# Attention and two MLPs on one core: another order for the opening, and two joins of the first MLP rearranged

## The chip, the cores and the metric

The kernel runs on one core of a Trainium2 chip. The metric is the device time of one execution in microseconds (us), lower is better. It is one program: the time starts before the first load and ends with the last store.

## What is computed

Attention over 4 batches of 8 heads, 576 positions, head width 64, with a bias from a running sum; then a first MLP with a leaky activation (a slope alpha per hidden unit), then a second MLP with a squared relu. The result of each feeds the next.

```
scores = scale * q @ k.T
cum    = cumsum(maximum(s, 0))                       # over the sequence
scores = where(causal, -1e9, scores + minimum(-(cum_i - cum_j), 0))
attn   = exp(scores - max) / (sum + 1e-9)
x      = (attn @ v) as 2304 x 512
h = x @ w_in  (512 -> 2048);  g = maximum(h, 0) + alpha * minimum(h, 0);  y = g @ w_out  (2048 -> 512)
h = y @ w_in2 (512 -> 2048);  g = maximum(h, 0) ** 2;                     out = g @ w_out2
```

## The kernel before

**Number format.** Every fp32 operand of a matmul is split into a rounded part `hi` and a rest `lo` (`hi` L323, `lo` L335 for q and k; L985 and L986, L624, L610, L668, L1369 and L1370, L1417 and L1418 elsewhere). A product is the sum of three matmuls (hi*hi, hi*lo, lo*hi; the table `TERMS`). So each tile that TensorE reads has been made by one instruction for hi (mostly ScalarE or GpSimd) and one for lo (mostly VectorE or GpSimd).

**Attention.** The 16 pairs of heads run as a pipeline. For a pair: `load_qk`, split, transposes on TensorE into the bank `ps_tr` (`pp` L344 for a head of q or k, 4 transposes each; `pp_tail` L369 for the last 64 positions; in a later pair two `pp` stand together as 8), evacuation to QS, QM (q, scaled), KS, KH (k) by ScalarE or VectorE, scores by `qk` (L412; row tile i and head h, operations `qk_ih`; matmuls L419, L420, L425), `red` on VectorE (L446: mask and row maximum), `exp` on ScalarE (L459), transposes of the probabilities (`tr`, L527), and two products with v (L561, L577). The score matmul of 66 rows (L420) reads, beside k, two rows of KH that hold the running sum `cum`; they come by a DMA, for pair 0 straight from the split sum `cum_hl` (tile `pt`), for later pairs by way of the DRAM tensor `cumD`.

**Opening.** L691 to L772 write the order of pair 0's loads, splits, transposes and evacuations by hand, with the splits of pair 1 (raw_q_132, raw_k_133 in the order rows; pair 0 has raw_q_123, raw_k_124). `s` arrives in the tile `prl`; `cum` is a relu (L711) and a scan (L712) on VectorE. `init_persistent` (L269) zeroes the tail columns of QM, QS and other tiles: for pair 0 on VectorE (L271 to L273, and the memset of `cum` L710) and partly GpSimd, for pair 1 on GpSimd. `keep_warm` (L696) issues filler matmuls of zeros (tile `iv`) into the bank `ps_xa`; they compute nothing that is used. From pair 0's scores on, the table `PIPE` gives each operation a slot in a pair, `RAMP` shifts operations of the first (and last) pairs by fractions of a pair, `WARM` puts filler matmuls of 256 columns ahead of operations of pair 0. The sum of slot and shift sorts all operations, and `in_order` chains the instructions of each engine in that order.

**First MLP.** Three passes over thirds of the 2304 rows (768 each, in halves of 384). Passes 0 and 1 are steps 0 to 15 and 16 to 31: a step makes 128 hidden units (`mlp_mm` L637; activation and split `mlp_act` L658 to L668 in tiles gg and gs) and adds their share of the outputs (`mlp_parts` L922, matmuls L935, in four portions of six matmuls, one called a chunk here). The third pass, `pass_of_seven` (L1373), makes 2 x 2 blocks by seven products instead of eight (L1440, a product is six matmuls; z = 0 to 6 counts them, q = 0 to 7 the groups), and places one chunk behind each product:

```
                in_order(IN_ORDER[:1])
                if (q<7) or (z>1):
                    chunk()
                in_order(IN_ORDER[:1])
```

The chunks of group q = 0 are still the outputs of steps 30 and 31. The third pass needs sums of x (tile xc, split at L985 and L986, differences L1020, handed out as `handed` steps) and sums of weights. These weight sums (`prep_sums` L181 to L184, `prep_first` L196 to L199, and the conversions `prep_conv` L133 to L142) are a list of tasks `todo` that is dealt out over the steps by `spans`, triples of first step, last step and share of the tasks' cost (L964).

## Time and profile before

| | |
|---|---|
| runs, us | 950.13, 950.86 (median), 954.41 |
| profiled execution, us | 952.03 |
| its span, us | 950.2 |
| mean granted TensorE clock | 1.000 |
| TensorE busy | 936.9 us, 99% of the span |

The span counts from the first to the last instruction, the profiled execution 1.9 us more. Times in the views are counted from the start of the span. A row of a timeline gives start and busy time; consecutive equal instructions stand in one row with their count; in brackets the idle time ahead of it and what ended that.

### The profile page before, as it was taken

How to read it: one execution, taken by the hardware profiler on the slowest of the kernel's cores; microseconds unless marked ns; L12 is line 12 of the kernel's file. 1: busy time of each engine (PE TensorE's matmuls, PEld its weight loads, DVE VectorE, ACT ScalarE, POOL GpSimd, SP SyncE). 2: the span in 40 equal slices, each digit the busy share in tenths (PEclk: the TensorE clock that was granted, in tenths of full speed). 3: DMA queues.
4: the chain of work that ended last, by engine and by line, in shares of the span. 5: the costliest groups of instructions: out<-in, count | busy, mean ns of one | idle time of the engine just before them, and what ended most of it. 6: DMA issues, size and time to landing. Idle time of an engine off the chain costs nothing.

```text
span 950.2 us, 16991 instructions
## 1 busy us (share of the span) xinstructions
PE 936.9 (99%) x5909; PEld 882.6 (93%) x5909; DVE 770.4 (81%) x1446; ACT 607.1 (64%) x1272; POOL 280.3 (29%) x278
## 2 busy tenths in 40 slices
PE   7999999999999999999999999999999999999998
PEld 6888888899999899999999999999999999999998
DVE  7788878868778987789778878788988888888685
ACT  6999988856566565577666656566445664456432
POOL 7466555134233212322102100344003530045200
PEclk9999999999999999999999999999999999999999
DMA  5787765337666758989568562586755867448384
GB/s 148 197 210 205 198 156 139 87 103 252 208 198 228 275 192 301 341 276 311 168 214 261 184 200 82 163 314 217 244 182 164 273 222 261 146 118 287 118 259 134
DMA packets 141063, 195.69 MB, mean 206 GB/s; under 512 B 50962, under 2 KB 102674, under 8 KB 135602
## 3 DMA queue, kind: packets, MB, share of 16 engines
q1 hardware_dynamic: 140384, 194.11, 65.1%
q8 instruction: 47, 0.77, 0.3%
q10 hardware_dynamic: 594, 0.50, 0.2%
q14 instruction: 38, 0.31, 0.1%
HBM read 140.47 MB, written 45.83 MB: 196 GB/s over the span
## 4 chain that ended last, share of the span: by engine, by line
PE 91%; DVE 3%; DMA 2%; ACT 1%; SPq 1%; issue 1%; POOL 0%; ACTq 0%; DVEq 0%; POOLq 0%
PE acc L1253 18%; PE po L935 18%; PE ph L637 12%; PE ph L1440 6%; PE a L1094 5%; PE b L1094 5%; PE c L1094 5%; PE ps_tr L527 5%; PE ps_xb L577 3%; PE d L1094 3%; PE ps_xa L561 2%; PE ps_sc L419 2%; PE ps_sc L420 2%; PE ps_tr L348 2%; PE ps_sc L425 2%; DMA raw_w<-in_moe_w_in_dram 1%
## 5 line engine op out<-in xcount | busy, mean ns | idle before, releaser
L1253 PE MATMUL acc<-th,w2s 128*128 128x384 f32 x1008 | 177.6, 335 | 0.0
L1253 PEld LDWEIGHTS acc<-th,w2s 128*128 128x128 f32 x1008 | 175.2, 188 | 0.0
L935 PE MATMUL po<-gs,wo_hi 128*128 128x512 f32 (+1 forms) x768 | 166.3, 336 | 0.7 <-DVE gs L1418 0.5
L935 PEld LDWEIGHTS po<-gs,wo_hi 128*128 128x128 f32 x768 | 122.8, 188 | 14.3 <-DVE gs L1418 1.1
L637 PE MATMUL ph<-xs,wi_hi 128*128 128x384 f32 x512 | 130.6, 335 | 2.1 <-DVE gg L664 1.9
L985 ACT CAST th<-g 128x768 fp32r<-128x768 f32 x84 | 70.2, 836 | 78.5 <-PE acc L1253 57.0
L986 DVE TENSOR_TENSOR th<-g,th 128x768 fp32r<-128x768 f32 x84 | 80.2, 955 | 24.8 <-ACT th L985 24.6
L935 PE MATMUL po<-gs,wo_lo 128*128 128x256 f32 (+1 forms) x384 | 99.1, 337 | 0.0
L637 PEld LDWEIGHTS ph<-xs,wi_hi 128*128 128x128 f32 x512 | 90.6, 188 | 4.0 <-DVE gg L664 2.7
L986 DVE TENSOR_TENSOR w1h<-w1f,w1h 128x512 fp32r<-128x512 f32 x96 | 74.3, 777 | 22.2 <-ACT w1h L985 22.0
L142 POOL TENSOR_TENSOR wc<-cv_t,wc 128x512 uint32<-128x512 uint32 x24 | 37.0, 1549 | 165.3 <-DVE cv_t L138 121.1
L637 PE MATMUL ph<-xs,wi_lo 128*128 128x384 f32 x256 | 85.6, 334 | 0.0
L985 ACT CAST w1h<-w1f 128x512 fp32r<-128x512 f32 x96 | 53.8, 565 | 39.6 <-PE b L1094 25.4
L446 DVE CUSTOM_DVE_ANT_0 pr<-ps_sc,mask 128x128 f32<-128x128 f32 (+3 forms) x128 | 61.8, 486 | 14.3 <-PE ps_sc L420 11.3
L142 POOL TENSOR_TENSOR wf<-cv_t,wf 128x512 uint32<-128x512 uint32 x32 | 45.2, 1413 | 94.3 <-DVE cv_t L138 71.0
L1105 POOL TENSOR_TENSOR g<-g 128x384 f32<-128x384 f32 x24 | 23.8, 990 | 162.2 <-ACT g L1104 162.1
L459 ACT ACTIVATE pr<-pr,nmax 128x128 f32<-128x128 f32 (+3 forms) x128 | 71.2, 557 | 0.4
L935 PEld LDWEIGHTS po<-gs,wo_lo 128*128 128x128 f32 x384 | 59.2, 188 | 7.9
L1094 PE MATMUL a<-xc,w1h 128*128 128x384 f32 x288 | 58.5, 335 | 0.0
L1440 PE MATMUL ph<-xc,wi_hi 128*128 128x384 f32 x224 | 57.6, 337 | 0.6 <-DVE xc L986 0.6
L1094 PE MATMUL c<-xc,w1h 128*128 128x384 f32 x288 | 58.0, 334 | 0.0
L1094 PE MATMUL b<-xc,w1h 128*128 128x384 f32 x288 | 57.8, 335 | 0.0
(204 smaller groups left out, 2130.2 us busy)
## 6 DMA issues: line engine op xcount, KB each, us to landing
w2s<-w2D SPq DMA_DIRECT2D x42, 1024.0 KB
w1f<-w1D SPq DMA_DIRECT2D x72, 256.0 KB
raw_w<-in_moe_w_in_dram SPq DMA_DIRECT2D x32, 512.0 KB
w2D<-whl SPq DMA_DIRECT2D x16, 896.0 KB
raw_w<-in_moe_w_out_dram SPq DMA_DIRECT2D x24, 512.0 KB
...
```

The lines of the kernel that those rows point to most:

```text
L142: nc.gpsimd.tensor_tensor(d, tt, d, ALU.add)
L446: nc.vector.tensor_tensor_reduce(o, banks.pop(("s", i, h))[:, :w], m, -1.0, first, ALU.add, ALU.min, nmax[:, h : h + 1])
L459: nc.scalar.activation(o, o, AF.Exp, bias=m, scale=-1.0, accum_out=sums_of[n][:, i, h : h + 1])
L527: last = nc.tensor.transpose(ps[:, z * P : (z + 1) * P], pr[:, c0 : c0 + P], ident)
L577: last = nc.tensor.matmul(xb[64 * h : 64 * h + 64, c0 : P + TAIL], vv[:, j, h, :], pt[:, h, j, c0:], start=(j == 0), stop=(j == 4),)
L637: nc.tensor.matmul(ph[h][:, :HT], ws[a][:, kb * P : (kb + 1) * P], xs[kb][:, bb, h * HT : (h + 1) * HT], start=(cnt == 0), stop=(cnt == 3 ...
L935: nc.tensor.matmul(acc, ws[a][:, m * P : (m + 1) * P], gs[:, bb, c_], start=first_ and z == 0, stop=lst and z == 2, skip_group_check=True,)
L985: a = nc.scalar.copy(dst[:, 0], src)
L986: v = nc.vector.tensor_sub(dst[:, 1], src, dst[:, 0].bitcast(F32))
L1094: nc.tensor.matmul(pt[:, :HT], hl[:, a, c0 + kb * P : c0 + (kb + 1) * P], xc[i][:, b, kb, :], start=(first and cnt == 0), stop=(cnt == 5), ...
L1253: nc.tensor.matmul(acc[m][:, :HT], ws[:, y, (2 * q + qq) % 4, m * P : (m + 1) * P], th[:, x, qq, :], start=(fresh and q == 0 and qq == 0 a ...
L1440: nc.tensor.matmul(acc[:, :HT], hl[a][:, c0 + kb * P : c0 + (kb + 1) * P], xp[i][:, b, kb, :], start=(fresh and cnt == 0), stop=(cnt == 5) ...
```

## The change

**1. The opening** is written in another order. The tails of q and k (64 positions) are loaded by DMAs of their own on ScalarE's queue, the main parts both on SyncE's queue (SP); k of pair 1 is loaded ahead of q; v of pair 0 ahead of the two rows of KH; the store to `cumD` goes to ScalarE's queue. The memsets of QM, QS and `cum` leave VectorE (three of them are GpSimd's; the scan starts from the zero tile). The splits of pair 0 are dealt out anew: hi of q, of k's second head and of k's tail on ScalarE, hi of k's first head on GpSimd; lo of k's first head, of k's tail and of q's heads on VectorE, lo of k's second head and of q's tail on GpSimd. The transposes of pair 0 run k, q, k, tails, q; three of the filler matmuls of 512 columns behind the first block go away, and one of the first block. GpSimd takes lo of pair 1's k before that of its q, with beta (L71, made from alpha) between them. In the diff, the long old sequence is left out; it is in the code above.

```diff
+    H0, H1, HT_ = slice(0, 4), slice(4, 8), slice(8, 9)
+    nc.vector.memset(zero, 0.0)
+    nc.gpsimd.memset(ptl[0][0:64, :, 4, :], 0.0)
+    load_main(0, 0, nc.sync)
+    nc.scalar.dma_start(s_sb, s.rearrange("b h c -> (b h) c"))
+    load_main(0, 1, nc.sync)
+    nc.vector.memset(warm, 0.0)
+    nc.gpsimd.memset(QM[0].bitcast(F32)[:, :, 0:TAIL], 0.0)
+    keep_warm(8)
+    nc.gpsimd.memset(raw_v[0][0:64, 4, :, :], 0.0)
+    nc.vector.tensor_scalar(s_sb, s_sb, 0.0, None, ALU.max)
+    load_tail(0, 0, nc.scalar)
+    nc.vector.tensor_tensor_scan(cum, s_sb, zeros, 0.0, ALU.add, ALU.add)
+    load_qk(1, 1, nc.sync)
+    load_tail(0, 1, nc.scalar)
+    nc.gpsimd.memset(QS[0].bitcast(F32)[:, :, 0:TAIL], 0.0)
+    hi(0, 1, 2, H0)
     hi(0, 0, 0, H0)
...
+    load_qk(1, 0, nc.sync)
+    hi(0, 1, 0, H1)
+    nc.scalar.copy(cum_hl[:, 0, :], cum)
+    hi(0, 1, 0, HT_)
+    keep_warm(1)
+    lo(0, 1, 1, H0)
+    nc.gpsimd.memset(QM[0].bitcast(F32)[64:66, :, TAIL:], 1.0)
+    load_v(0)
+    lo(0, 0, 1, H0)
+    pp(0, 1, 0)
+    nc.gpsimd.memset(rs_[0], 0.0)
+    hi(0, 0, 0, slice(4, 9))
     lo(0, 1, 2, H1)
+    lo(0, 0, 2, HT_)
+    nc.scalar.activation(warm, warm, AF.Exp)
+    pp(0, 0, 0)
+    pp(0, 1, 1)
+    nc.vector.tensor_sub(cum_hl[:, 1, :], cum, cum_hl[:, 0, :].bitcast(F32))
+    ks_out(0, 0)
+    nc.sync.dma_start(KH[0].bitcast(F32)[64:66, 0, :], cum_hl.bitcast(F32)[0 : 1])
+    hi(1, 1, 2)
+    hi(1, 0, 2)
+    keep_warm(2)
+    nc.scalar.dma_start(cumD, cum_hl.bitcast(F32))
...
+    lo(1, 1, 2)
+    load_alpha()
...
+    lo(1, 0, 2)
```

The engine operand of `hi` and `lo` is 0 for ScalarE, 1 for VectorE, 2 for GpSimd.

**2. RAMP and WARM** have new numbers: the shifts of most operations of pairs 0 to 2 and of some of pair 3 change by up to a pair and mostly by under a fifth of one. The fillers are now

```diff
-    WARM = {("qk_11", 0): 1, ("qk_20", 0): 2, ("qk_21", 0): 3, ("qk_30", 0): 3, ("qk_31", 0): 2, ("qk_40", 0): 2, ("tr_0", 0): 1, ("tr_1", 0): 1}
+    WARM = {('qk_20', 0): 4, ('qk_21', 0): 2, ('qk_30', 0): 2, ('tr_0', 0): 2, ('tr_1', 0): 4, ('qk_01', 0): 1, ('qk_00', 0): 1, ('pp_q0', 1): 1}
```

**3. The join of passes 0 and 1.** The spans of the weight tasks move a little, which takes one `prep_first` (four subtractions) from step 15 to step 17 and shifts single tasks in steps 18 to 22.

```diff
-    spans = ((13,14.3,.11),(16.6,29.2,.65),(33.5,43,.24))
+    spans = ((13, 13.9, 0.09), (16.3, 29.2, 0.67), (33.5, 43, 0.24))
```

**4. The join of pass 1 and the third pass.** In the last step (31) one more input step is issued ahead of the activation, and the chunks of group q = 0 stand otherwise: two behind product z = 0, one behind z = 1 and z = 3, the rest after the group.

```diff
+        if step == len(steps) - 1:
+            with tc.issue_after(anchor), tc.issue_after(anchor_v):
+                for _ in range(1):
+                    handed.pop(0)()
         gs, anchor, anchor_v = mlp_act(f, ph, step == 0)
...
-                if (q<7) or (z>1):
+                for _ in range(2*(z==0)+(z in(1,3)) if q==0 else int(q<7 or z>1)):
                     chunk()
```

**In the built order.** On TensorE at the very start, before the change (hl_q and hl_k are the split q and k, ps_xa the bank of the fillers, KS to QM the transposed operands of pair 0):

```order
L348 MATMUL ps_tr<-ident_r,hl_q 128x128 x4
L700 MATMUL ps_xa<-iv 128x512
L348 MATMUL ps_tr<-ident_r,hl_k 128x128 x4
L700 MATMUL ps_xa<-iv 128x512
L348 MATMUL ps_tr<-ident_r,hl_q 128x128 x4
L700 MATMUL ps_xa<-iv 128x512
L348 MATMUL ps_tr<-ident_r,hl_k 128x128 x4
L700 MATMUL ps_xa<-iv 128x512
L373 MATMUL ps_tr<-ident_r,hl_q 128x128
L373 MATMUL ps_tr<-ident_r,hl_k 128x128
L700 MATMUL ps_xa<-iv 128x512 x2
```

and after it:

```order
L348 MATMUL ps_tr<-ident_r,hl_k 128x128 x4
L348 MATMUL ps_tr<-ident_r,hl_q 128x128 x4
L348 MATMUL ps_tr<-ident_r,hl_k 128x128 x4
L700 MATMUL ps_xa<-iv 128x512 x2
L373 MATMUL ps_tr<-ident_r,hl_q 128x128
L373 MATMUL ps_tr<-ident_r,hl_k 128x128
L348 MATMUL ps_tr<-ident_r,hl_q 128x128 x4
L700 MATMUL ps_xa<-iv 128x512
L419 MATMUL ps_sc<-KS_121,QS_119 128x128
L420 MATMUL ps_sc<-KH_122,QM_120 128x128
L700 MATMUL ps_xa<-iv 128x256
```

The first head of k now stands ahead of q's, the first three blocks of transposes follow one another with no filler between, and the second head of q comes last.

On VectorE at the start, before (prl is s and then its running sum, pt the split sum, L726 and L318 evacuate):

```order
L692 MEMSET iv 128x576
L706 MEMSET warm 1x1
L271 MEMSET QM_120 2x2x576
L272 MEMSET QM_120 66x2x64
L273 MEMSET QS_119 128x2x64
L710 MEMSET prl 32x576
L711 TENSOR_SCALAR prl<-prl 32x576
L712 SCALAR_TENSOR_TENSOR prl<-prl 32x576
L338 TENSOR_TENSOR hl_q<-raw_q_123,hl_q 128x4x64
L338 TENSOR_TENSOR hl_q<-raw_q_123,hl_q 128x5x64
L744 TENSOR_TENSOR pt<-prl,pt 32x576
```

and after:

```order
L738 MEMSET iv 128x576
L743 MEMSET warm 1x1
L747 TENSOR_SCALAR prl<-prl 32x576
L749 SCALAR_TENSOR_TENSOR prl<-prl,iv 32x576
L338 TENSOR_TENSOR hl_k<-raw_k_124,hl_k 128x4x64
L338 TENSOR_TENSOR hl_q<-raw_q_123,hl_q 128x4x64
L772 TENSOR_TENSOR pt<-prl,pt 32x576
L338 TENSOR_TENSOR hl_k<-raw_k_124,hl_k 128x64
L338 TENSOR_TENSOR hl_q<-raw_q_123,hl_q 128x4x64
L318 CAST KS_121<-ps_tr 128x512
```

The four memsets between `warm` and the relu are gone; behind the scan the lo of k's first head has come in ahead of q's, and a lo of k's tail behind the running sum.

On TensorE behind the last step of pass 1, before (L1440 is a product of the third pass, L935 a chunk of step 30's outputs, the numbers those of banks and input tiles):

```order
L1440 MATMUL ph<-xc_5750,wi_hi 128x384 x2
L1440 MATMUL ph<-xc_5750,wi_lo 128x384
L1440 MATMUL ph<-xc_5750,wi_hi 128x384 x2
L1440 MATMUL ph<-xc_5750,wi_lo 128x384
L935 MATMUL po_4878<-gs,wo_hi 128x512
L935 MATMUL po_4882<-gs,wo_hi 128x256
L935 MATMUL po_4878<-gs,wo_hi 128x512
L935 MATMUL po_4882<-gs,wo_hi 128x256
L935 MATMUL po_4878<-gs,wo_lo 128x512
L935 MATMUL po_4882<-gs,wo_lo 128x256
L1440 MATMUL ph<-xc_5752,wi_hi 128x384 x2
L1440 MATMUL ph<-xc_5752,wi_lo 128x384
```

and after (L1471 and L962 are the same lines):

```order
L1471 MATMUL ph<-xc_5750,wi_hi 128x384 x2
L1471 MATMUL ph<-xc_5750,wi_lo 128x384
L962 MATMUL po_4878<-gs,wo_hi 128x512
L962 MATMUL po_4882<-gs,wo_hi 128x256
L962 MATMUL po_4878<-gs,wo_hi 128x512
L962 MATMUL po_4882<-gs,wo_hi 128x256
L962 MATMUL po_4878<-gs,wo_lo 128x512
L962 MATMUL po_4882<-gs,wo_lo 128x256
L962 MATMUL po_4879<-gs,wo_hi 128x512
L962 MATMUL po_4882<-gs,wo_hi 128x256
L962 MATMUL po_4879<-gs,wo_hi 128x512
L962 MATMUL po_4882<-gs,wo_hi 128x256
```

The second chunk has moved from behind the second product to ahead of it.

## Rows read from the trace of the kernel before

**Rows 1.** The page: span, TensorE's busy time, and its busy tenths in 40 slices.

```profile
span 950.2 us, 16991 instructions
...
PE 936.9 (99%) x5909; PEld 882.6 (93%) x5909; DVE 770.4 (81%) x1446; ACT 607.1 (64%) x1272; POOL 280.3 (29%) x278
...
PE   7999999999999999999999999999999999999998
```

**Rows 2.** Windows: busy us of each engine, granted clock, DMA share, GB/s.

```profile
0.00:25.00 25.00, 19.07 (x123) 16.02 (x123) 18.07 (x51) 15.82 (x41) 18.05 (x35) 1.00 0.60 150
...
25.00:50.00 25.00, 25.00 (x223) 21.85 (x221) 19.84 (x68) 22.84 (x74) 12.13 (x12) 1.00 0.73 196
```

**Rows 3.** Timeline of TensorE, 0 to 25 us: start, us, instruction, [idle before <-releaser].

```profile
2.22 3.86 PE L700 MATMUL ps_xa<-iv 128*128 128x512 f32 x10 [2.22 <-DVE warm L706]
...
6.78 0.53 PE L348 MATMUL ps_tr<-ident_r,hl_q 128*128 128x128 f32 x4 [0.69 <-DVE hl_q L338]
...
9.66 0.53 PE L348 MATMUL ps_tr<-ident_r,hl_k 128*128 128x128 f32 x4 [0.84 <-POOL hl_k L338]
...
13.70 0.88 PE L348 MATMUL ps_tr<-ident_r,hl_k 128*128 128x128 f32 x8 [0.91 <-POOL hl_k L338]
...
19.84 0.50 PE L419 MATMUL ps_sc<-KS,QS 128*128 128x512 f32 x1 [0.69 <-DVE nmax L446]
...
22.39 0.82 PE L527 MATMUL ps_tr<-ident,pr 128*128 128x128 f32 x6
...
22.96 0.30 PE L419 MATMUL ps_sc<-KS,QS 128*128 128x128 f32 x1
```

**Rows 4.** Timeline of VectorE, 0 to 25 us.

```profile
2.49 1.02 DVE L271 MEMSET QM<- 2x1152 f32 x1 [0.32 <-issue]
...
4.41 0.39 DVE L711 TENSOR_SCALAR prl<-prl 32x576 f32<-32x576 f32 x1
...
4.83 1.58 DVE L712 TENSOR_TENSOR_SCAN prl<-prl 32x576 f32<-32x576 f32 x1
```

**Rows 5.** DMA of 0 to 25 us: GB/s in 40 slices of 0.625 us.

```profile
GB/s 0 0 10 96 334 385 240 213 143 203 213 40 42 42 32 21 7 103 164 210 163 69 5 17 213 187 111 206 228 145 297 292 104 44 129 217 325 374 245 121
```

**Rows 6.** Timeline of GpSimd, 0 to 25 us.

```profile
5.30 2.02 POOL L338 TENSOR_TENSOR hl_k<-raw_k,hl_k 128x256 fp32r<-128x256 f32 x1
...
8.74 0.86 POOL L338 TENSOR_TENSOR hl_k<-raw_k,hl_k 128x320 fp32r<-128x320 f32 x1
...
12.24 1.41 POOL L338 TENSOR_TENSOR hl_k<-raw_k,hl_k 128x576 fp32r<-128x576 f32 x1
...
15.80 0.20 POOL L71 TENSOR_SCALAR beta_sb<-alpha_sb 128x16 f32<-128x16 f32 x1
```

**Rows 7.** Timeline of SyncE's queue (SP), 0 to 25 us.

```profile
12.35 0.59 SPq L70 DMA_DIRECT2D alpha_sb<-in_moe_alpha_dram  x1
```

**Rows 8.** Timelines of TensorE and VectorE at the end of step 15 and behind it.

```profile
322.98 0.61 PE L637 MATMUL ph<-xs,wi_hi 128*128 128x384 f32 x2 [1.95 <-DVE gg L664]
...
320.93 1.48 DVE L184 TENSOR_TENSOR wc<-wc 128x256 f32<-128x256 f32 x1
...
322.85 0.41 DVE L196 TENSOR_TENSOR w0s<-wf 128x256 f32<-128x256 f32 x1
...
330.94 1.07 PE L637 MATMUL ph<-xs,wi_hi 128*128 128x384 f32 x3
```

**Rows 9.** Timelines of TensorE and VectorE after step 31.

```profile
462.01 0.85 PE L935 MATMUL po<-gs,wo_hi 128*128 128x512 f32 x4
...
463.07 0.33 PE L1440 MATMUL ph<-xc,wi_hi 128*128 128x384 f32 x1
...
464.00 0.44 PE L1440 MATMUL ph<-xc,wi_hi 128*128 128x384 f32 x1 [0.60 <-DVE xc L986]
...
463.00 1.82 DVE L986 TENSOR_TENSOR xc<-xT,xc 128x768 fp32r<-128x768 f32 x2
...
477.45 0.62 PE L935 MATMUL po<-gs,wo_hi 128*128 128x512 f32 x2 [0.48 <-DVE gs L1418]
```

More of the change, by code (lines that the diff above doesn't have):

```diff
@@ L691, in attention_then_two_mlps @@
     zero = apool.tile([P, S], F32, name="iv", tag="iv", bufs=1)
-    nc.vector.memset(zero, 0.0)
-    zero = zero.bitcast(F32R)
-    blank = [None]
+    zeros, blank = zero[0:BH], [None]
+    warm = apool.tile([1, 1], F32, name="warm", bufs=1)
     def keep_warm(k, cols=512):
@@ L698, in keep_warm, with load_main, load_tail @@
             blank[0] = ps_x.tile([P, 512], F32, name="ps_xa", tag="ps_x")
+        z = zero.bitcast(F32R)
         for _ in range(k):
-            nc.tensor.matmul(blank[0][:, :cols], zero[:, 0:P], zero[:, :cols], start=True, stop=True)
-    nc.scalar.dma_start(s_sb, s.rearrange("b h c -> (b h) c"))
-    load_qk(0, 0)
-    load_qk(0, 1, nc.scalar)
-    warm = apool.tile([1, 1], F32, name="warm", bufs=1)
-    nc.vector.memset(warm, 0.0)
-    nc.scalar.activation(warm, warm, AF.Exp)
-    keep_warm(10)
-    init_persistent(0)
-    nc.vector.memset(cum, 0.0)
-    nc.vector.tensor_scalar(s_sb, s_sb, 0.0, None, ALU.max)
-    nc.vector.tensor_tensor_scan(cum, s_sb, cum, 0.0, ALU.add, ALU.add)
-    for x in range(2):
-        load_qk(1, x)
+            nc.tensor.matmul(blank[0][:, :cols], z[:, 0:P], z[:, :cols], start=True, stop=True)
+    def load_main(n, x, e):
+        b, hp = pairs[n]
+        e.dma_start(
+            raw_qk[x][n % 2][:, 0:8, :].rearrange("p (h t) d -> p h (t d)", h=2),
+            (q, k)[x][b, 2 * hp : 2 * hp + 2][:, 0 : 4 * P].rearrange("h (p t) d -> p h (t d)", t=4),
+        )
+    def load_tail(n, x, e):
+        b, hp = pairs[n]
+        e.dma_start(raw_qk[x][n % 2][:, 8, :], (q, k)[x][b, 2 * hp : 2 * hp + 2][:, 4 * P : S])
     def kview(a, c):
@@ L734, in attention_then_two_mlps @@
-    H0, H1 = slice(0, 4), slice(4, 9)
-    hi(0, 0, 0, H0)
-    hi(0, 0, 0, H1)
-    hi(0, 1, 2, H0)
-    lo(0, 1, 2, H0)
-    hi(0, 1, 2, H1)
-    lo(0, 1, 2, H1)
-    nc.scalar.copy(cum_hl[:, 0, :], cum)
-    lo(0, 0, 1, H0)
-    lo(0, 0, 1, H1)
-    nc.vector.tensor_sub(cum_hl[:, 1, :], cum, cum_hl[:, 0, :].bitcast(F32))
-    for h in range(2):
-        for x in range(2):
-            pp(0, x, h)
-            keep_warm(1)
-    qs_out(0, 0)
-    for h in range(2):
-        nc.sync.dma_start(KH[0].bitcast(F32)[64:66, h, :], cum_hl.bitcast(F32)[h : h + 1])
@@ L752, in attention_then_two_mlps, with scaled, qs_out @@
-    nc.sync.dma_start(cumD, cum_hl.bitcast(F32))
-    load_v(0)
-    kh_out(0, 0, 0)
-    qm_out(0)
-    kh_out(0, 0, 1)
-    kh_out(0, 1, 2)
-    qs_out(0, 1)
-    kh_out(0, 1, 1)
-    qm_out(1)
-    pp_tail(0)
-    keep_warm(2)
+    def scaled(dst, src, e):
+        if e == 0:
+            nc.scalar.activation(dst, src, AF.Copy, scale=SCALE)
+        else:
+            nc.vector.tensor_scalar(dst, src, SCALE, None, ALU.mult)
+    def qs_out(n, h, e):
+        scaled(kview(QS[n][:, h, P:], "p (c t) -> p c t"), bank_of(0, h), e)
@@ new lines, in qm_out, with ks_out, kh_out @@
+    def qm_out(h, e):
+        scaled(kview(QM[0][0:64, h, P:], "p (c t) -> p c t"), bank_of(0, h)[0:64], e)
+    def ks_out(h, e):
+        evac(kview(KS[0][:, h, 0 : 4 * P], "p (c t) -> p c t"), bank_of(1, h), e)
+    def kh_out(h, e):
+        evac(kview(KH[0][0:64, h, 0 : 4 * P], "p (c t) -> p c t"), bank_of(1, h)[64:128], e)
+    H0, H1, HT_ = slice(0, 4), slice(4, 8), slice(8, 9)
+    nc.vector.memset(zero, 0.0)
+    nc.gpsimd.memset(ptl[0][0:64, :, 4, :], 0.0)
+    load_main(0, 0, nc.sync)
@@ new lines, in attention_then_two_mlps @@
+    ks_out(0, 0)
[4 more added lines that the diff above has]
+    nc.scalar.dma_start(cumD, cum_hl.bitcast(F32))
+    kh_out(0, 0)
+    lo(0, 1, 1, HT_)
+    pp_tail(0)
+    lo(0, 0, 1, H1)
+    ks_out(1, 1)
+    pp(0, 0, 1)
+    keep_warm(1)
+    kh_out(1, 0)
+    nc.sync.dma_start(KH[0].bitcast(F32)[64:66, 1, :], cum_hl.bitcast(F32)[1 : 2])
+    lo(1, 1, 2)
+    load_alpha()
+    qs_out(0, 1, 0)
+    qs_out(0, 0, 1)
@@ L763, in attention_then_two_mlps @@
+    qm_out(1, 0)
+    lo(1, 0, 2)
+    qm_out(0, 1)
     q_tail(0)
+    init_persistent(1)
+    load_v(1)
     k_tail(0)
-    for x in range(2):
-        hi(1, x, 2)
-    for x in range(2):
-        lo(1, x, 2)
-    init_persistent(1)
-    load_alpha()
-    load_v(1)
     PIPE = (
```

10 lines of the change are left out of this document (1 added, 9 removed).

## The prediction

> **What bounds the kernel now.** I read the page first: TensorE is busy for 936.9 of 950.2 us, and of the 40 slices of its busy tenths only the first (7) and the last (8) lie below 9 [rows 1]. A change that takes no work from TensorE can therefore gain only where TensorE still stands idle, so I looked for those places. The windows put most of them in the first 25 us: TensorE is busy for 19.07 of 25.00 us there, and for 25.00 of 25.00 in the next window [rows 2]. Of the 5.93 us idle, 2.22 come before the first filler matmul [rows 3]; that wait for VectorE's zero tile and warm stays as it is, which leaves 3.71 us. TensorE's timeline shows the long waits that remain, with what ended them: 0.84 us ahead of k's second head at 9.66 and 0.91 us ahead of pair 1's k at 13.70, both for the rest of k made by GpSimd, and 0.69 us each ahead of the first transposes (6.78) and of a score matmul at 19.84 [rows 3]. The other two places that the change touches are single stalls of TensorE: 1.95 us at the end of step 15 [rows 8], and 0.60 and 0.48 us behind step 31 [rows 9].
>
> The profiled execution took 952.03 us, 1.17 over the median 950.86. I make the sum against 952.03 and take the difference off the median, since nothing in the change depends on what lies around the span. 0.5% is 4.75 us, about what a measurement of this kernel can tell from no change: faster begins below 946.1, slower above 955.6.
>
> **The opening, step by step.**
>
> *First transposes.* Before, they start at 6.78 because VectorE makes the rest of q only after the memsets (the first 1.02 us), the relu at 4.41 and the scan from 4.83 to 6.41 [rows 4]. With the memsets gone, VectorE is free when the warm tile is done, near 2.2, and the relu waits for s. The trace has no row for the landing of s. It cannot be before VectorE is free, and by the old order it was there at 4.41, so the scan ends between 4.2 and 6.4. The transfer row gives 10, 96, 334 and 385 GB/s from 1.25 to 3.75 us [rows 5], that is some 275 kB by 3.1 and 515 kB by 3.75; s (72 kB) was issued beside the first loads, so I take 3.5 for the relu and 5.5 for the end of the scan. The rest of k's head 0 follows on VectorE, between 0.41 (VectorE's subtraction of as many elements, L196 [rows 8]) and GpSimd's 0.86 [rows 6]; I take 0.65, and k's transposes start at about 6.25, q's at 6.9. Gain 0.5 of the old 0.69; nothing if s lands late.
>
> *k's second head.* It came at 9.66, behind GpSimd's chain of hi, lo (2.02 us, from 5.30), a wait for the tail and lo (0.86) [rows 3, 6]. Now ScalarE makes its hi, and GpSimd goes from the hi of head 0 (over near 5.2) through a memset of QM of about 1 us, taken over from VectorE, and a small one to this lo. Started near 6.5 it takes 0.86 to 2.02, so the transposes can go at 7.4 to 8.5; I take 7.9, since VectorE runs its own subtractions beside it. The price of such company shows in the same rows: 2.02 us for 256 columns, 0.86 for 320. The Trainium skill, page "SBUF — State Buffer", section "Who interferes with whom", says that VectorE and GpSimd share one pair of ports as an exclusive lock, so that of two such instructions one is blocked for the whole of the other; by it the 7.9 would become the 8.5 of the long row, and the sum 0.6 us poorer.
>
> *First scores and pair 1's k.* The filler matmuls behind the first block fall from six of 512 columns to three, and q's second head now stands last, so the first scores come about 0.7 us sooner. Before, pair 1's k was held to 13.70 by GpSimd, whose lo of it ran from 12.24 to 13.65 [rows 3, 6]. Now GpSimd has neither the lo of k's head 0 nor the hi of its second head, and takes k ahead of q: lo of k's head 1 to about 7.9, hi of k and q of pair 1 and one small lo to about 9.5, lo of k (1.41) to about 10.9. TensorE gets there after two scores of head 0 and one of head 1, at about 11.9. So this point moves from 13.70 to 11.9, −1.8.
>
> *From there to pair 1's first score.* Before it took 22.96 − 13.70 = 9.26 us [rows 3]. After, ten of the transposes of probabilities that stood before it come behind it (six take 22.96 − 22.39 = 0.57, so ten 1.0), one score matmul of 256 columns comes in (0.25) and there is one filler more (0.12). The wait of 0.69 at 19.84 was for a row maximum; in the new order twelve transposes and four fillers stand ahead of that score, so I take it as gone. 9.26 − 1.0 + 0.25 + 0.12 − 0.69 = 7.9, so pair 1 starts at 19.8; with the ten transposes still to do that is like 20.8 before. **Opening: 22.96 − 20.8 = −2.1.** Bounds: 0, if the chain is held elsewhere (rival C); at best all 3.71 us of idle go, and the fillers change by four of 512 columns less and two of 256 more. A chunk of 2304 columns takes 1.06 us, from 462.01 to 463.07 [rows 9], so 512 columns take 0.24 and 256 take 0.12: −0.7, together −4.4.
>
> *Beta.* GpSimd makes beta from alpha at 15.80 with no wait; alpha was issued at 12.35, so it landed within 3.45 us [rows 6, 7]. Now beta stands ahead of the lo of pair 1's q, so a late alpha would hold that and the memsets and splits of pair 2 behind it. Alpha is issued behind the rows of KH, which wait for the split sum at about 7.6, hence at about 9.5, and is there by 13.0 at the latest; lo of q then ends by 14.6, and TensorE reaches q's transposes at about 14.3. Cost 0, up to 0.3.
>
> *Other moves.* On SP, the rows of KH now stand behind v, and the load of raw weights ahead of the KH rows of pair 1; both cost their issue time (0.59 us for a row of this queue [rows 7]), covered by TensorE's fillers and scores; without that cover up to 0.6 each. The exps that move behind evacuations are hidden while TensorE has transposes to do.
>
> *Pairs 1 to 4.* The second window has no idle [rows 2], so the shifted numbers of RAMP can give nothing that shows there and may cost something: 0, bounds −1.0 and +1.5.
>
> **Join of passes 0 and 1.** The stall of 1.95 us ends with VectorE's activation (L664), which stands behind the sum L184 that took 1.48 us, against 0.41 for an equal subtraction (L196) a moment later [rows 8]. In the changed program VectorE's order up to and with this L664 is the same; only the four subtractions behind it leave, 0.41 each. So the stall stays. A step later TensorE shows a small gap: three matmuls of one row take 1.07, where the two behind the stall take 0.61 and a third adds 0.18 by its columns [rows 8], so 0.28 too long; with 1.6 us less on VectorE ahead of it I take it as gone. **−0.3**, bounds 0 and −0.4. If the sum L184 were after all freed of its company, 1.07 more.
>
> **Join of pass 1 and the third pass.** The second matmul of product z = 1 … 3 waits for VectorE's split: the third product's first matmul starts at 463.07, its second at 464.00, 0.75 later than the 0.18 that its columns take [rows 9]. Two chunks behind z = 0 put 1.06 us of work (462.01 to 463.07) ahead, and the split (1.82 for two, from 463.00) is now issued one step sooner. The second stall, ahead of a chunk of the third pass at 477.45, waits for that pass's first gs; with the four chunks of step 31 all behind the group, gs has 3 more chunks' time. I count 0.75 + 0.63 (its 0.48 and the 0.15 by which the first exceeded its own 0.60) − 0.1 left over. **−1.3**, bounds −0.5 (one stall merely moves to a product without a chunk) and −1.4.
>
> **Sum.** −2.1 − 0.3 − 1.3 = −3.7: the profiled execution at 948.3, the median at **947.2**.
>
> **The rivals.** *A, the forecast:* 947.2, from 945.4 to 948.6. *B, the opening loses nearly all its idle:* if the chain of splits stays ahead of TensorE throughout, −4.4 and joins −1.8: −6.2, 944.6. For it: two thirds of the idle are single waits for splits that the change reorders. Against it: these waits sit on chains that go through all engines, and the scan alone is 1.58. *C, the opening gives nothing:* s or k's tail lands late, ScalarE (now making four hi's, the copy of cum and issuing three loads) holds the evacuations, and only −1.6 of the joins is left: 949.3. For it: ScalarE waits on k's tail in its order. *D, the joins give nothing* and the opening −2.1: 948.8. *E, slower:* TensorE's clock falls during the new opening. The first ten fillers take 3.86 us, where ten of 512 columns would take 2.4 at the chunk's pace: a start that looks like the lower of the two levels (1.2 GHz), with the granted clock of the window still at 1.00 [rows 2, 3]. If the thinner opening (9 and 3 fillers instead of 10 and 6) leaves TensorE at that level from 6.25 to 19.8, its work there is doubled: before, it was busy for 15.2 us (19.07 − 3.86) in the 18.2 behind the first transposes, so some 11 in these 13.6. Against the gain of 3.7 that is +7.3, 958.2. It decides against the kernel from about 3.7 us of work at the lower level. Against it: waits of 0.84 and 0.91 did not do it before, and the new ones are no longer. The Trainium skill, page "TensorE: Matmul & The Clock Gate", section "HAM oscillation — how this bites in real kernels", says that a TensorE left idle is set back to half its clock and pays the warm-up again; by that rule E is the case to fear, and the granted 1.00 of this trace does not show it.
>
> **How the numbers follow.** A 0.42, B 0.24, C 0.20, D 0.08, E 0.06. The range 943.4 to 950.1 takes in A, C, D and B with up to a further 1 us for pairs 1 to 4; out of it are E and the edges of B and C, some 0.15. Faster by over 0.5% (below 946.1): B and 0.17 of A's lower end, 0.41. Slower by over 0.5%: E, 0.06. The rest, 0.53, is within 0.5%.
>
> **What would show it.** Right: TensorE's first transposes near 6.3, pair 1's k near 11.9, pair 1's first score near 19.8, no wait of TensorE for xc or gs behind step 31, the 1.95 us at step 15 still there. Wrong: a relu that starts at 4 or later, GpSimd idle ahead of beta, ScalarE's evacuations late behind a tail, a wait in 25 to 125 us that was not there, transposes and scores of the opening at twice their times, or the stall of step 15 gone.

## The result and the profile after

The changed kernel takes 959.31 us (median of 8 runs, 955.74 to 961.5), the kernel before 950.64 (median of 8, 949.95 to 954.41): the ratio is 1.0081, interval 1.0065 to 1.0096. The forecast was 947.2 with a range of 943.4 to 950.1. The kernel became slower, and the time lies outside the range. Two executions far from all others, one of 1867.61 us in run e8 and one of 2189.76 us of the kernel before, are left out of the medians and ratios below.

The page of the changed kernel, to be read beside [rows 1]: span, TensorE's busy time, its busy tenths and its granted clock in 40 slices.

```profile
span 958.4 us, 16984 instructions
...
PE 942.9 (98%) x5907; PEld 887.8 (93%) x5907; DVE 766.9 (80%) x1444; ACT 607.7 (63%) x1274; POOL 281.7 (29%) x280
...
PE   8899999999999999999999999999999999999998
...
PEclk8999999999999999999999999999999999999999
```

The span is 8.2 us longer, and only 2.2 of that is idle time (958.4 − 942.9 = 15.5 against 950.2 − 936.9 = 13.3). The other 6.0 are busy time, though two matmuls fewer are recorded: the same work ran longer. The clock row says why for the first slice: it stands at 8, where the windows of [rows 2] have 1.00. The second slice of TensorE has fallen to 8; in [rows 1] it was full. The windows say where (columns as in [rows 2]).

```profile
0.00:25.00 25.00, 20.90 (x117) 18.13 (x117) 15.95 (x48) 15.70 (x42) 19.23 (x39) 0.86 0.64 162
25.00:50.00 25.00, 20.29 (x169) 17.18 (x169) 16.85 (x55) 18.39 (x57) 9.43 (x10) 0.97 0.58 151
...
12.00:18.00 6.00, 6.00 (x32) 6.00 (x31) 3.14 (x12) 3.05 (x10) 4.06 (x9) 0.50 0.83 182
...
50.00:52.00 2.00, 2.00 (x16) 1.50 (x14) 0.00 (x0) 2.00 (x8) 1.92 (x2) 0.50 0.43 135
332.00:334.00 2.00, 2.00 (x8) 2.00 (x7) 2.00 (x5) 2.00 (x4) 0.00 (x0) 0.51 0.87 344
```

Two things are new. The window from 25 to 50, which had no idle time at all [rows 2], has 4.71 us of it. And in three places the granted clock is 0.50 or 0.51, the lower level of 1.2 GHz. TensorE's waits, with their releasers (total us, times, longest):

```profile
PE ps_tr L348 <- POOL hl_k L338: 5.1, 2, 4.7
...
PE ph L637 <- DVE gg L664: 1.9, 1, 1.9
PE ps_sc L420 <- DMA KH<-pt: 1.2, 1, 1.2
```

The two stalls behind step 31 [rows 9] are gone from this list, and so is the wait for a row maximum [rows 3]. New are one wait of 4.7 us for a k split of GpSimd and one of 1.2 us for rows of KH; a third, of 0.78 us, comes at 88.44, for rows of KH of a later pair. TensorE's timeline shows the first two in their places, with the points that the prediction named.

```profile
6.22 0.72 PE L348 MATMUL ps_tr<-ident_r,hl_k 128*128 128x128 f32 x4
...
7.81 0.54 PE L348 MATMUL ps_tr<-ident_r,hl_k 128*128 128x128 f32 x4 [0.35 <-POOL hl_k L338]
...
11.64 0.44 PE L420 MATMUL ps_sc<-KH,QM 66*128 66x128 f32 x1 [1.24 <-DMA KH<-pt]
...
13.27 1.18 PE L348 MATMUL ps_tr<-ident_r,hl_k 128*128 128x128 f32 x8
...
22.41 0.31 PE L419 MATMUL ps_sc<-KS,QS 128*128 128x128 f32 x1
...
48.78 0.75 PE L348 MATMUL ps_tr<-ident_r,hl_k 128*128 128x128 f32 x4 [4.71 <-POOL hl_k L338]
49.46 2.94 PE L577 MATMUL ps_xb<-ptl,raw_v 128*64 128x192 f32 x20
...
331.14 0.62 PE L637 MATMUL ph<-xs,wi_hi 128*128 128x384 f32 x2 [1.87 <-DVE gg L664]
...
340.63 0.68 PE L637 MATMUL ph<-xs,wi_hi 128*128 128x384 f32 x3
```

The wait at 48.78 leads to GpSimd, whose timeline holds the main finding:

```profile
7.03 0.72 POOL L338 TENSOR_TENSOR hl_k<-raw_k,hl_k 128x256 fp32r<-128x256 f32 x1
...
13.82 0.20 POOL L71 TENSOR_SCALAR beta_sb<-alpha_sb 128x16 f32<-128x16 f32 x1 [1.88 <-DMA alpha_sb<-in_moe_alpha_dram]
...
28.38 1.41 POOL L338 TENSOR_TENSOR hl_q<-raw_q,hl_q 128x576 fp32r<-128x576 f32 x1
44.58 1.04 POOL L505 TENSOR_TENSOR x<-x,iv 128x384 f32<-128x384 f32 x1 [14.79 <-DMA iv<-sD]
...
46.59 0.66 POOL L333 TENSOR_SCALAR hl_k<-raw_k 128x576 fp32r<-128x576 f32 x1
47.33 1.40 POOL L338 TENSOR_TENSOR hl_k<-raw_k,hl_k 128x576 fp32r<-128x576 f32 x1
```

From 28.38 + 1.41 on GpSimd does nothing for 14.79 us: it stands at the normalisation of pair 0 (L505), which needs the inverse sums `iv` back from memory. Behind it in the same queue stand hi and lo of pair 4's k (46.59, 47.33), and for that lo TensorE waits. The same place in the trace of before, on GpSimd and on TensorE, rows on which the prediction didn't draw:

```profile
32.34 0.67 POOL L333 TENSOR_SCALAR hl_k<-raw_k 128x576 fp32r<-128x576 f32 x1
33.09 1.42 POOL L338 TENSOR_TENSOR hl_k<-raw_k,hl_k 128x576 fp32r<-128x576 f32 x1
...
47.39 1.01 POOL L505 TENSOR_TENSOR x<-x,iv 128x384 f32<-128x384 f32 x1 [0.44 <-DMA iv<-sD]
```

```profile
42.97 0.46 PE L348 MATMUL ps_tr<-ident_r,hl_k 128*128 128x128 f32 x4
...
44.26 1.64 PE L577 MATMUL ps_xb<-ptl,raw_v 128*64 128x192 f32 x20
```

The split ran first, at 32.34 and 33.09, the normalisation behind it, and TensorE reached these transposes at 42.97 without a wait. The entry `('nrm', 0): -0.79` of RAMP, which shifts the due time of pair 0's normalisation, carried it past the split. SyncE's queue in the changed kernel shows when the data could come at all:

```profile
4.32 3.70 SPq L298 DMA_DIRECT2D raw_v<-in_v_dram  x2
8.06 0.76 SPq L301 DMA_DIRECT2D raw_v<-in_v_dram  x1
8.95 0.67 SPq L774 DMA_DIRECT2D KH<-pt  x1
...
10.30 0.40 SPq L70 DMA_DIRECT2D alpha_sb<-in_moe_alpha_dram  x1
...
16.57 0.99 SPq L105 DMA_DIRECT2D raw_w<-in_moe_w_in_dram  x1
17.60 0.62 SPq L397 DMA_DIRECT2D KH<-cumD  x1
...
40.46 1.23 SPq L497 DMA_DIRECT2D iv<-sD  x2
```

The load of `iv` is issued at 40.46 and ends GpSimd's wait at 44.58. No place of the normalisation on GpSimd's queue makes that earlier; an earlier place of the load itself on SyncE's queue was not tried. ScalarE and VectorE in the opening and at the first join:

```profile
2.38 0.52 ACTq L711 DMA_DIRECT2D raw_k<-in_k_dram  x1
...
7.69 0.24 ACT L329 CAST hl_k<-raw_k 128x64 fp32r<-128x64 f32 x1 [1.50 <-DMA raw_k<-in_k_dram]
```

```profile
3.62 0.48 DVE L747 TENSOR_SCALAR prl<-prl 32x576 f32<-32x576 f32 x1 [1.45 <-DMA prl<-in_s_dram]
4.13 1.34 DVE L749 TENSOR_TENSOR_SCAN prl<-prl,iv 32x576 f32<-32x576 f32 x1
...
329.08 1.48 DVE L184 TENSOR_TENSOR wc<-wc 128x256 f32<-128x256 f32 x1
```

### The profile page after: what moved, and what is told of

It reads as the page before. It is cut to its first block, busy times and chain, and to the rows that moved or that the text cites. A ratio compares the mean times of both kernels' runs of the same rounds, so it can differ in the third digit from the quotient of the medians.

```text
span 958.4 us, 16984 instructions
## 1 busy us (share of the span) xinstructions
PE 942.9 (98%) x5907; PEld 887.8 (93%) x5907; DVE 766.9 (80%) x1444; ACT 607.7 (63%) x1274; POOL 281.7 (29%) x280
## 4 chain that ended last, share of the span: by engine, by line
PE 92%; DMA 3%; DVE 2%; issue 1%; ACT 1%; POOL 0%; SPq 0%; ACTq 0%; DVEq 0%; POOLq 0%
PE po L962 19%; PE acc L1280 18%; PE ph L637 12%; PE ph L1471 6%; PE a L1121 5%; PE b L1121 5%; PE c L1121 5%; PE ps_tr L527 5%; PE d L1121 3%; PE ps_xb L577 3%; PE ps_sc L419 2%; PE ps_xa L561 2%; PE ps_sc L420 2%; PE ps_tr L348 2%; PE ps_sc L425 2%
## 5 line engine op out<-in xcount | busy, mean ns | idle before, releaser
L962 PE MATMUL po<-gs,wo_hi 128*128 128x512 f32 (+1 forms) x768 | 166.9, 337 | 0.0
L962 PEld LDWEIGHTS po<-gs,wo_hi 128*128 128x128 f32 x768 | 123.2, 189 | 13.8 <-DVE gs L668 0.6
L962 PE MATMUL po<-gs,wo_lo 128*128 128x256 f32 (+1 forms) x384 | 99.2, 337 | 0.0
L459 ACT ACTIVATE pr<-pr,nmax 128x512 f32<-128x512 f32 (+3 forms) x128 | 71.1, 556 | 1.5 <-DVE nmax L446 1.3
L962 PEld LDWEIGHTS po<-gs,wo_lo 128*128 128x128 f32 x384 | 59.2, 188 | 7.9
L1471 PE MATMUL ph<-xc,wi_hi 128*128 128x384 f32 x224 | 57.5, 337 | 0.1
```

The source lines that it names most:

```text
L459: nc.scalar.activation(o, o, AF.Exp, bias=m, scale=-1.0, accum_out=sums_of[n][:, i, h : h + 1])
L962: nc.tensor.matmul(acc, ws[a][:, m * P : (m + 1) * P], gs[:, bb, c_], start=first_ and z == 0, stop=lst and z == 2, skip_group_check=True,)
L1471: nc.tensor.matmul(acc[:, :HT], hl[a][:, c0 + kb * P : c0 + (kb + 1) * P], xp[i][:, b, kb, :], start=(fresh and cnt == 0), stop=(cnt == 5) ...
```

## The experiments

The theory after reading the trace: the place of pair 0's normalisation costs nearly all of the loss, and the opening's gain was eaten by late transfers. The rival: TensorE at half its clock in the opening (E of the prediction, whose 958.2 lies close to the result) costs it. Ratios are to the kernel before, timed beside each run, with 95% intervals; where medians of two different calls are subtracted, the ratios beside them say how far that holds.

### The normalisation taken back, and put into the kernel before

**e1_norm_back** is the changed kernel without one number of the table; only GpSimd's order changes.

```diff
-    RAMP = {... ('lo_k', 1): 0.33, ('nrm', 0): -0.79, ('dk', 0): -0.18, ...}
+    RAMP = {... ('lo_k', 1): 0.33, ('dk', 0): -0.18, ...}
```

> The changed kernel with one number of RAMP taken back (the norm of pair 0, -0.79), which puts GpSimd's norm of pair 0 behind the split of pair 4's k again and moves nothing else on any engine. If the norm's place caused TensorE's wait of 4.7 us at 48.8 us, that wait goes and with it the stretch at half clock behind it: 952.5 to 954. If the late landing of the norm's factors would have held TensorE anyway by another way, the time stays within 1.5 us of the changed kernel's 959.3.

Measured: 950.59 us, ratio 0.9996 (0.9985 to 1.0007). One number of the table costs 8.7 us in the medians (959.31 − 950.59), 8.1 by the two ratios, more than the 5.3 to 6.8 that was expected. GpSimd's timeline has the split back at its old time, and the normalisation finds its data there:

```profile
29.55 0.67 POOL L333 TENSOR_SCALAR hl_k<-raw_k 128x576 fp32r<-128x576 f32 x1
30.30 1.43 POOL L338 TENSOR_TENSOR hl_k<-raw_k,hl_k 128x576 fp32r<-128x576 f32 x1
...
47.21 1.02 POOL L505 TENSOR_TENSOR x<-x,iv 128x384 f32<-128x384 f32 x1
```

The half clock of the opening is still there in this kernel:

```profile
10.00:16.00 6.00, 5.59 (x28) 5.31 (x29) 4.21 (x14) 4.70 (x14) 5.07 (x7) 0.50 0.68 120
```

So the rival falls as the cause of the loss: six microseconds at the lower level, and the time is that of before. TensorE has another wait here that the kernel before has not, 1.40 us at 82.15, ahead of a score matmul (L420) and put down to a DMA; the 0.78 of the changed kernel stands ahead of such a matmul too. No run isolates what brings them.

**e5_norm_first_in_before** is the reverse: the kernel before, with the normalisation moved ahead of the same split. The orders of TensorE, VectorE and ScalarE stay; on SyncE's queue one store of weights (L200) moves ahead of a load of v.

```diff
-    RAMP = {...}
+    RAMP = {..., ("nrm", 0): -0.5, ("di", 0): -0.15, ("hi_k", 4): 0.28, ("lo_k", 4): 0.27}
```

> The kernel before, with four numbers of RAMP that put GpSimd's norm of pair 0 ahead of the split of pair 4's k, as the changed kernel has it; TensorE, VectorE and ScalarE keep their order, and on SyncE's queue one store of weights moves. If that place alone makes the loss, TensorE waits some 5 us near 46 us for pair 4's k here too, and the time is 957 to 960. If the loss needs the rest of the new opening, 950.5 to 952.

Measured: 961.43, ratio 1.0102 (1.0082 to 1.0122), a little above the expected range. Its timelines of TensorE and of GpSimd repeat the picture of the changed kernel:

```profile
48.49 0.75 PE L348 MATMUL ps_tr<-ident_r,hl_k 128*128 128x128 f32 x4 [5.38 <-POOL hl_k L333]
```

```profile
46.26 0.99 POOL L505 TENSOR_TENSOR x<-x,iv 128x384 f32<-128x384 f32 x1 [13.60 <-DMA iv<-sD]
```

The granted clock is 0.50 from 48 to 54 us here too. The move is enough by itself, without the new opening and without the joins. A table of where the first four blocks of the product `xa` (L561) start on TensorE, read from the timelines, shows where the time is lost and that it isn't given back:

```text
                 first   second  third   fourth
before           27.42   38.74   50.10   62.53
changed          28.13   38.96   56.91   69.34
e1_norm_back     27.84   38.65   50.13   62.56
e5               27.40   38.72   58.63   71.08
e10_all_links    26.60   37.42   48.90   61.55
```

Between the second and the third block the changed kernel loses 56.91 − 50.13 − 0.31 = 6.5 us against e1: 4.71 of waiting, and behind it matmuls at the lower clock (the 20 of `xb` at 49.46 take 2.94, in e1 and before 1.64). The profiled spans of the two differ by 958.4 − 948.6 = 9.8; a further 1.7 of that comes from a second stretch at half clock, behind the stall of step 15 (332 to 336 at 0.51 and 0.63), and 0.7 because that stall is 1.87 there and 1.15 in e1. These last two are no consequence that the runs tie to the normalisation. Of the rest, 0.3 was lost before the second block, and 0.6 is not accounted for.

### The joins alone

**e4_joins_only** is the kernel before with the three edits of the joins.

```diff
-    spans = ((13,14.3,.11),(16.6,29.2,.65),(33.5,43,.24))
+    spans = ((13, 13.9, 0.09), (16.3, 29.2, 0.67), (33.5, 43, 0.24))
...
+        if step == len(steps) - 1:
+            with tc.issue_after(anchor), tc.issue_after(anchor_v):
+                for _ in range(1):
+                    handed.pop(0)()
...
-                if (q<7) or (z>1):
+                for _ in range(2*(z==0)+(z in(1,3)) if q==0 else int(q<7 or z>1)):
```

> The kernel before with parts 3 and 4 of the change alone (spans, input step, chunks); its opening is the old one. By my sum -1.6: 949.0 (948.8 to 950.0), with the stall of 1.95 us at step 15 still there and the two behind step 31 gone. If the joins cost something themselves, as by the half clock that the changed kernel shows behind step 15: 951 to 953.

Measured: 949.97, ratio 0.9986 (0.9975 to 0.9996): 1.2 us shorter in the medians, where −1.6 was forecast. TensorE's stall of step 15 is 1.5 us in its profile, the waits for xc and gs behind step 31 are gone. With e1 this gives the worth of the new opening with the other shifts of RAMP: 950.59 − 949.97 = +0.6 instead of −2.1, and not distinguishable from zero by the two intervals.

**e11_join2_only** is the kernel before with the last two of these edits (the second join alone).

> The kernel before with part 4 alone (input step and chunks). By my sum -1.3, 949.8 where the kernel before gives 951.2; if the spans bring the gain of the joins, no change.

Measured: 951.2, ratio 1.0002 (0.9989 to 1.0016). The two stalls are gone from its trace, but the time isn't shorter. Its mean clock over the runs is 0.9973, that of before in the same call 0.998; whether that hides the gain can't be told from these runs. The expected 949.8 was missed, and why stays open.

These two kernels have the old opening, and in their profiled executions the granted clock falls there too: to 0.50 from 14 to 16 us and 0.73 from 16 to 18 in e4, to 0.54 and 0.60 in e11. In e11 the wait ahead of it is the old one for pair 1's k, 0.90 us at 13.30. So the lower level is no mark of the new opening; in the one profile of the kernel before it merely did not occur.

### The links of the opening, one by one

A link is here a load, a split or a row that comes late and at which a wait of TensorE ends.

**e2_kh_first** is the changed kernel with v loaded behind the rows of KH.

```diff
-    load_v(0)
     lo(0, 0, 1, H0)
...
     lo(1, 1, 2)
+    load_v(0)
     load_alpha()
```

> The changed kernel with the load of pair 0's v moved behind the two rows of the running sum on SyncE's queue. If these rows came late because they stand behind v, TensorE's wait of 1.24 us for them goes, and if that wait is what took the clock to half from 12 to 18 us, about 3 us more: 954.5 to 956. If the clock falls because the whole opening is thin (fewer fillers), the wait goes but the half clock stays: 957.5 to 958.5. If the rows are late by their own transfer, nothing moves.

Measured: 957.73, ratio 1.0065 (1.0042 to 1.0087). The wait for KH is gone. The median is 1.6 us below that of the changed kernel, but the intervals of the two ratios overlap widely, so a gain is not shown; and the transposes of the tails (L373) now wait on TensorE, 1.46 us ahead of 10.55, for GpSimd's lo of q's tail. The edit doesn't touch the tails: k's tail came later here than in the profile of the changed kernel, and let ScalarE go at 9.26 instead of 7.69. In e1, e3, e6 and e9, which load the tails in the same way, it is 9.09, 8.81, 8.84 and 8.97. So 7.69 was the early case, and in the other profiles without fillers ahead of the tails (e1, e2, e3) the first long wait is that of the tails.

**e3_fill_kh** puts six more filler matmuls ahead of the first score, to keep TensorE busy while it waits for KH.

```diff
     pp(0, 0, 1)
-    keep_warm(1)
+    keep_warm(7)
     kh_out(1, 0)
```

> The changed kernel with six fillers of 512 columns more ahead of the first score matmul, which cover TensorE's wait of 1.24 us for the rows of the running sum; the wait's cause stays. If idle time is what takes the clock down at 12 us, the granted clock stays at full and the time falls by some 2 to 3.5 us: 955.5 to 957.5. If the clock falls for another reason, the time is the same or up to 1 us longer: 959 to 960.5.

Measured: 956.86, ratio 1.0056 (1.0038 to 1.0074), inside the range expected if the clock stays up; yet in the profiled execution it fell, so the number does not bear that reading out. The fillers came too late there: the tails wait here too (1.21 us ahead of 10.10), and the seven fillers behind them already began at the lower clock: they took 3.31 us, where the ten of e6 took 2.56 at the upper level. That execution is the longest of the eight, 959.54 at a mean clock of 0.994; the three with 0.998 or more took 953.56 to 954.76, still 2.4 to 3.6 us above the 951.16 of the kernel before.

The next four start from e1. **e6_fill_tails** has eight fillers more ahead of the tails' transposes; **e7_tail_sp** issues the tails of q and k on SyncE's queue behind the main parts, instead of on ScalarE's; **e8_tail_sp_kh_first** is e7 with the move of e2; **e9_fill_tails_kh1_first** is e6 with the rows of KH of pair 1 issued ahead of the raw weights (the entry `('dk', 1): 0.15` of RAMP taken out).

```diff
     hi(1, 0, 2)
-    keep_warm(2)
+    keep_warm(10)
     nc.scalar.dma_start(cumD, cum_hl.bitcast(F32))
```

```diff
     load_main(0, 1, nc.sync)
+    load_tail(0, 1, nc.sync)
+    load_tail(0, 0, nc.sync)
...
-    load_tail(0, 0, nc.scalar)
...
-    load_tail(0, 1, nc.scalar)
```

> The first experiment's kernel (norm back in its place) with eight fillers of 512 columns more ahead of the transposes of the tails, to cover TensorE's wait of 1.5 us there. If the idle time is what takes the clock to half from 10 to 17 us, the clock stays at full and the time falls to 947.5 to 949.5. If the clock falls all the same, 950.5 to 952.

Measured: 952.08 (948.39 to 957.37), ratio 1.0012 (0.9995 to 1.003); the gain was missed. The profiled run, the shortest, has a granted clock of 1.00 from 10 to 20 us, and what comes out next is pair 1's first score, whose second matmul waits 1.64 us for KH<-cumD at 22.10.

The times of its runs tend to follow the mean clock: 948.39 and 949.04 at 1.0, 953.07 and 955.84 at 0.996, 957.37 at 0.994; one, 954.26 at 0.999, doesn't fit in.

> The first experiment's kernel with the loads of the tails of q and k on SyncE's queue behind the main parts, no longer on ScalarE's. If the late tail of k is what holds ScalarE (it waited 2.9 us for it) and behind it the evacuations, TensorE's wait of 1.5 us goes; the wait for the rows of the running sum may come back in part: 948.5 to 950. If the tails are late by the volume ahead of them, nothing moves: 950.5.

Measured: 951.75, ratio 1.0004 (0.9993 to 1.0014); the gain was missed here too. The tails' wait is gone; in its place stand 1.48 us for KH<-pt at the first score and 1.42 for KH<-cumD at pair 1's.

> As the one with the tails on SyncE's queue, and v of pair 0 behind the rows of the running sum. If tails and rows are the two links that hold the new opening, both waits go, the clock stays up and the forecast of the opening comes true: 947 to 948.5. If the opening is bound by something else, as the one with the tails alone.

Measured: 954.05 (median of 11 runs), ratio 1.0014 (0.9998 to 1.0031), far from the expected 947 to 948.5. KH<-pt is gone too, and the wait for KH<-cumD has grown to 2.08.

> The kernel with the norm back and eight fillers more ahead of the tails, and in it one more number of RAMP taken back (0.15 for the spreading of pair 1's k), which puts the running sum's rows of pair 1 ahead of the raw weights on SyncE's queue. If the 512 KB of weights ahead of them make these rows late, TensorE's wait of 1.64 us at 22 us goes and the time falls by 1.5 to 2.5 us against 952.1: 949.5 to 950.6. If they are late for the earlier loads or the store they read from, nothing moves.

Measured: 952.17, ratio 1.0005 (0.999 to 1.0019). The wait for KH<-cumD shrank from 1.64 to 0.6, a wait of 1.0 for QM<-QS came up, and the time didn't move. This expectation (949.5 to 950.6) was missed.

Each of these removes or shortens the wait that it aims at, and none gains anything clear: in each profile another late link stands behind it. So all were undone at once.

**e10_all_links** is e8 without `('dk', 1): 0.15` and with `keep_warm(6)` ahead of the tails. **e12_links_no_fill** is e10 with `keep_warm(2)` there, as in the changed kernel. **e13_links_fill_w_first** is e10 with `('dk', 1): 0.15` put back, so that the raw weights go first.

> The changed kernel with every link undone that a trace has shown: norm of pair 0 back, tails on SyncE's queue, v behind the rows of pair 0, rows of pair 1 ahead of the raw weights, four fillers more ahead of the tails. If these links are what holds the new opening, 947 to 948.5, better than the kernel before and the one with the joins alone (950.0). If each link undone brings forth the next, 950 to 953.

Measured: 949.19 (946.92 to 951.55), ratio 0.9978 (0.9965 to 0.9992): shorter than both kernels, and the only version from the new opening that is shorter than before beyond its interval. Its mean clock is 0.998 or more in all eleven runs. The expected 947 to 948.5 was not reached, and e10 contains the joins: against the joins alone (e4, 0.9975 to 0.9996) it is 0.8 us shorter in the medians of two calls, with overlapping intervals. So that the new opening gains anything of its own is not shown. SyncE's queue and TensorE's timeline:

```profile
7.17 0.65 SPq L773 DMA_DIRECT2D KH<-pt  x1
...
17.13 1.46 SPq L397 DMA_DIRECT2D KH<-cumD  x1
18.64 0.39 SPq L105 DMA_DIRECT2D raw_w<-in_moe_w_in_dram  x1
```

```profile
12.25 0.88 PE L348 MATMUL ps_tr<-ident_r,hl_k 128*128 128x128 f32 x8 [0.32 <-POOL hl_k L338]
...
20.52 0.31 PE L419 MATMUL ps_sc<-KS,QS 128*128 128x128 f32 x1
21.31 0.30 PE L420 MATMUL ps_sc<-KH,QM 66*128 66x128 f32 x1 [0.48 <-DMA KH<-cumD]
```

> The kernel with every link undone, without its four added fillers. If those fillers are what holds the granted clock through the new opening, the clock falls in most executions again and the time is 951.5 to 953.5. If the order of the loads alone makes the gain, 949 to 950.

Measured: 949.55, ratio 0.9989 (0.9978 to 1.0), the range expected if the order of the loads alone makes the gain. In the profiled execution, one of its longer ones with 951.15, the granted clock is 0.50 from 14 to 16 us all the same.

> The kernel with every link undone and its four fillers, but the raw weights ahead of pair 1's rows of the running sum again. If the late rows (a wait of 2.1 us at 22 us without fillers) are what cost, by idle time and by the clock behind it, 951 to 953. If the fillers alone make the gain, 949 to 950.

Measured: 951.42, ratio 1.0006 (0.999 to 1.0022), as expected if the late row costs. The same score waits five times as long with the weights ahead of the row:

```profile
22.82 0.30 PE L420 MATMUL ps_sc<-KH,QM 66*128 66x128 f32 x1 [2.41 <-DMA KH<-cumD]
```

Against e10 the raw weights' place is worth 951.42 − 949.19 = 2.2 us by medians of two calls, the four fillers 949.55 − 949.19 = 0.4. By the ratios it is 0.28% and 0.11%. The intervals of e10 and e13 just touch, those of e10 and e12 overlap by about half, so the order of the weights is likely the larger share, and the fillers' is not shown.

## Why the prediction was wrong

**Pairs 1 to 4: the step that failed.** The prediction said that the shifted numbers of RAMP "can give nothing that shows there and may cost something: 0, bounds −1.0 and +1.5". It judged them by TensorE's idle time in that window, which was none. That says how much can be gained, not how much can be lost. The +1.5 had no row behind it and no rival carried it: the range ends at 950.1, where rival C with +1.5 would be at 950.8. What had to be read was GpSimd's queue: the moved normalisation waits for a transfer that ended no sooner than 44.5 us, and the operations that it passed were ready at 29. The measured price is +8.7 (e1) and some +10 (e5: 961.43 against 951.38 of the kernel before beside it), against an upper bound of 1.5. The prediction did name the sign, a wait in 25 to 125 us that was not there. Both numbers needed for it stood in the trace of before: the normalisation at 47.39 with a wait for `iv` ahead of it, and the transposes of pair 4's k at 42.97. An operation that can't run before about 47, put ahead of a split that is wanted by 43, makes TensorE wait 4 us or more. (The range's lower end has a slip besides: by its own terms, 950.86 − 6.2 − 1.0, it is 943.7 and not 943.4. Nothing hangs on it.)

**The opening: the first links right, the sum wrong.** Scan over at 5.5: measured 4.13 + 1.34 = 5.47. First transposes 6.25: 6.22. k's second head 7.9: 7.81. The lo of GpSimd took 0.72 and not the 2.02 of the long row; but VectorE was through with its own work at 7.13, just as it began, so the company that the long end needed wasn't there. What the Trainium skill's page "SBUF — State Buffer", section "Who interferes with whom", says of it was not put to the test here. From there it went off: pair 1's k at 13.27 instead of 11.9, its first score at 22.41 instead of 19.8. With the 1.0 that the prediction added for the ten transposes still to come this is like 23.4, 0.4 later than before, where 2.1 earlier was forecast. With all links undone (e10) it is 12.25 and 20.52, that is 1.4 earlier than before: on TensorE's timeline two thirds of the 2.1 come once the late links are gone. In the time of the whole kernel they are not shown, as said at e10.

**"Other moves", the term that was mis-sized.** They were to cost their issue time of 0.59 each, hidden. But the three loads of v kept SyncE's queue from 4.32 to 8.82, and the first row of KH, whose input VectorE finished near 7.1, was issued at 8.95; in e10 it goes at 7.17, and the score doesn't wait. That is the wait of 1.24. The raw weights ahead of pair 1's row cost 0.99 of issue in the changed kernel, 1.08 in e13. There the row is issued at 18.11 and the score starts at 22.82, after a wait of 2.41; in e10, with the row ahead of the weights, these are 17.13, 21.31 and 0.48. So the score starts 1.5 us sooner, and 1.0 of that is the earlier issue alone. The bound for such a move was 0.6, and TensorE did not cover it. What a moved transfer costs is when the next one lands.

**Rival C was the nearer one for the opening.** "ScalarE waits on k's tail in its order" stood there as its ground, and that is what happened: the tail, issued at 2.38, let ScalarE go at 7.69, after 1.50 us of waiting, in other profiles near 9, and then TensorE's transposes of the tails wait for it (1.50 us in e1). e7 shows it by taking it away: with the tail on SyncE's queue ScalarE goes on at 6.09 without a wait. C's price, though, was 949.3, that is nothing gained; the result without the normalisation, 950.59, lies 1.3 above it.

**Rival E: the right picture, the wrong extent and price.** TensorE did run at the lower level from 12 to 18 us, as E had it, and the forecast of E (958.2) is almost the measured time. That is coincidence: e1 has the same half clock and takes 950.59. E let the lower level last from 6.25 to 19.8 and doubled some 11 us of work. In the changed kernel the granted clock from 10 to 18 us is 0.57 on average, with 6.76 us of busy time, so at most some 3 us are lost by it (an estimate, 6.76 × 0.43 = 2.9). The profile of e6, which is e1 with fillers and kept the full clock, has a span of 946.2 against 948.6, 2.4 us less. Part of what the lower level costs is covered by the chain of splits and transfers, which is late as well: with the clock up, e6 shows a wait of 1.64 instead. The argument against E, that waits of 0.84 and 0.91 did not do it before, rested on one execution: e11 has the old opening, a wait of 0.90 at that place, and the clock at 0.54 behind it.

**Beta.** Alpha was to be there by 13.0 and came at 13.8, issued at 10.30 and not at 9.5; GpSimd waited 1.88 us. TensorE has no wait behind it in the changed kernel; e10 shows 0.8 for the lo of q that stands behind beta, so the bound of 0.3 was too low once nothing else was late.

**Join of passes 0 and 1.** The stall stays, as forecast: 1.87 (1.15 in e1, 1.51 in e4, for no reason that the runs show), behind the sum L184 of 1.48 as in [rows 8]. The small gap a step later is gone: three matmuls take 0.68 where they took 1.07. What the step didn't have is the half clock behind the stall in this profile.

**Join of pass 1 and the third pass.** Both stalls are gone, as forecast. Of the −1.6 for both joins 1.2 came (0.4 to 2.4 by the interval); of the second alone nothing could be measured, and why stays open. So does what exactly separates the executions of one and the same opening, which in e6 spread over 9 us.
